# First loads in another order, decay products on ScalarE, two weight units decoded in thirds, and two blocks of tokens taken in turn

## The chip, the cores and the metric

One core of a Trainium2 chip runs the whole kernel. The time is device microseconds (us) of one execution; the kernel before was timed in three runs, and a fourth execution was profiled. Engines are named as in the profile: PE (TensorE; PEld is its weight load), DVE (VectorE), ACT (ScalarE), POOL (GpSimd), SP (the engine that issues most DMAs).

## The reference

The input is a state-space attention layer (4 batches, 8 heads, 768 positions, head size 32, state size 16), then a gated dense layer, then a layer of 8 experts of which each token takes one.

```python
la = log(clip(a)); cum = cumsum(la)                    # per chunk of positions
M  = (C @ B.T) * exp(cum_i - cum_j) * causal
y  = M @ x + (C @ state) * exp(cum)
state = exp(sum(la)) * state + (B * exp(cum_last - cum)).T @ x
X  = y as [3072 tokens, 256]
Z  = ((X @ w_a) * (X @ w_b)) @ w_out                   # w_a, w_b: 256 x 1536, w_out: 1536 x 256
e  = argmax(Z @ w_gate); g = softmax(Z @ w_gate)[e] * sigmoid((Z @ w_output_gate)[e])
out = g * (relu(Z @ w1[e]) @ w2[e])
```

## The kernel before, in words

**Tiles and units.** The 3072 tokens are 24 tiles of 128. Tiles are grouped in blocks (`BLK`, 2 or 4 tiles); blocks 0 and 1 have two tiles each and share one pair of buffers `xh`, `xl`. The dense layer's 1536 inner columns are 12 slices of 128, here called weight units f = 0 to 11. A unit of work (m, f) is block m through slice f: `unit_a` (product `pa` with w_a), `unit_b` (product `pb` with w_b, then the elementwise product and its split into `gh` and `gl`), and later `unit_o` (product `px` with w_out). Each full-precision product is three matmuls, high by high, low by high and high by low (`mm3`). The list `phases` sets the order of the units: block 0 through f = 0 to 2, then blocks 0 and 1 mixed through f = 5, then blocks 2 and 3, and later f = 6 to 11.

**Attention tiles.** `attn_stages(t)` has four steps per tile: `tr` (PE transposes of B and C into `ptr`, ACT evacuates them to `cd` and `BT`), `cb` (PE scores `pcb`, or `pcx` for tile 0; DVE multiplies them by the masked decays `lm` into `mt`), and `ys` (PE `py` or `pyx`; ACT writes `xh`, DVE writes `xl` and the state `Sst`). The decays come from `decays`: DVE scans `a`, and small per-row products follow. `pairs` makes rows 4 to 7 of a tile `q`; `parts` makes the products `A`, `Eb` and `all` (96x4 or smaller) out of `T`; `ends` makes rows 1 to 3 of `q` from them. `ex` transposes rows of `q` on PE and ACT evacuates them into `EX`. `prep` scales B and C by rows of `EX` (`cp`, `Cq`, `Bq`) and makes `lm` by a select on POOL.

**Weights.** They arrive as 64-bit floats, a pair of 32-bit words each. `load_w(f)` issues three loads into one `raw` buffer (w_a, w_b, w_out; three such buffers rotate). `split_w(f)` decodes them in six pieces: `shifted` (ACT, `u`), `low3`, `sign`, `join` (DVE, `raw` and `t`), `hi_w` (ACT, `whi`) and `lo_w` (DVE, `wlo`). Unit 0 is decoded in thirds (256 columns for w_a, then w_b, then w_out); all the others in whole rows of 768 columns.

**What sets the order.** From the first load to the barrier (`tc.no_sync_barrier`) the order on ACT, DVE, POOL and PE is the order in which the code is written. Behind it a scheduler places the instructions of the main loop on each engine. The loop records work unit by unit: a `tick` after each part of a unit brings in attention steps at a rate `PACE`, background steps (`bgstep`, two a tick) and decode steps from the list `dq` at a rate `RATE`; a unit that needs a slice not yet in `decoded` first brings in decode steps until it is there. Each engine executes its own list strictly in order. SP's list holds the loads of B and C (`BCin`, two buffers), of x (`xin`, six buffers) and of weights, each waiting until its buffer is free.

Of the kernel before, what the change touches and what calls it, by code (L numbers as in the profile page):

```python
# [7 lines left out]
F32 = mybir.dt.float32  # L8
# [10 lines left out]
def kernel(  # L19
# [34 lines left out]
    PACE = [2, 2, 2, 2, 1]  # L54
# [111 lines left out]
    def load_bc(u, i):  # L166

        if i == 0:
            BCin[u] = wk.tile([P, 2, G, H, N], F32, tag="BCin", name="BCin")
        b, c = divmod(u * G + i, NCH)  # L170
        for j, src in ((1, B), (0, C)):
            nc.sync.dma_start(out=BCin[u][:, j, i],
                              in_=src[b, :, c * P:(c + 1) * P, :].rearrange("h p n -> p h n"))
# [17 lines left out]
    def decays(r):  # L191
# [88 lines left out]
    def prep(u):  # L280
# [16 lines left out]
        def mul(o, j, qn, eng=None):  # L297
            (eng or nc.gpsimd).tensor_tensor(out=st[o], in0=BCin[u][:, j], in1=bc(qn), op=ALU.mult)

        def lm(i, hf):  # L300
# [4 lines left out]
            for s in range(hf * SUB // 2, (hf + 1) * SUB // 2):  # L305
# [6 lines left out]
        return dict(new=new, cp=lambda: mul("cp", 0, 0), Cq=lambda e=None: mul("Cq", 0, 1, e),  # L312
                    Bq=lambda e=None: mul("Bq", 1, 2, e),
# [123 lines left out]
    def load_w(f):  # L437
        r = stg.tile([P, 3, DM * WD], U32 if wide else F32, tag="raw", name="raw")
        s = slice(f * P * WD, (f + 1) * P * WD)
        for j, src in ((0, w_a), (1, w_b)):  # L440
            v = src.bitcast(U32) if wide else src
# [3 lines left out]
        nc.sync.dma_start(out=r[:, 2, :], in_=v[f * P:(f + 1) * P, :])  # L445
        raws[f] = r

    def split_w(f):
# [7 lines left out]
        def wide_pieces(s):  # L456
# [36 lines left out]
        def narrow_pieces(s):  # L493
            w_ = lambda v: v.rearrange("p j d -> p (j d)")[:, s]

            def hi():
                nc.scalar.activation(out=w_(whi[:, f]), in_=w_(raws[f]), func=AF.Copy)

            def lo():
                V.tensor_tensor(out=w_(wlo[:, f]), in0=w_(raws[f]), in1=w_(whi[:, f]).bitcast(F32),  # L500
                                op=ALU.subtract)
                if s.stop == 3 * DM:
                    decoded.add(f)
# [7 lines left out]
        if f == 1:  # L511
            return ps
# [382 lines left out]
    with tc.manual_schedule(engines={ET.Activation, ET.DVE, ET.Pool, ET.PE}):  # L895
        load_a(0)
        load_bc(0, 0)
        consts_early()
        load_x(0)
        load_bc(0, 1)  # L900
        load_x(1)
        load_w(0)
# [14 lines left out]
        RATE = [1.2, 0.6, 0.3, 0.4, 0.8]  # L917
# [7 lines left out]
        dq = split_w(1) + [more_w]  # L925
# [83 lines left out]
        wa, wb, wo = first  # L1009
# [56 lines left out]
    phases = [(mf(0, range(3)), 1, ()),  # L1066
              ([(0, 3), (1, 0), (1, 1), (0, 4), (1, 2), (1, 3), (0, 5), (1, 4), (1, 5)], 2, ()),
# [102 lines left out]
    for n in range(NU + LAG):  # L1170
# [358 lines left out]
```

## Time and profile before

| | |
|---|---|
| three timed runs | 614.42, 617.46 (median), 619.43 us |
| profiled execution | 617.15 us, of which 615.5 us is the span from the first to the last instruction |
| mean granted TensorE clock | 0.985 of full speed |
| PE matmul busy | 572.7 us, 93% of the span |
| DVE, POOL, ACT busy | 331.1, 250.7 and 243.1 us |

Times in the trace count from the start of the span. In a row, the first numbers are start and duration; what stands in square brackets is how long the engine sat idle before it and whose result it waited for. "x8" means that eight instructions of the same kind are merged in a row, with their busy time together.

### The profile page before, as it was taken

The numbers are of one execution on the slowest core, as the hardware profiler recorded it, in microseconds if no ns is written. First come the engines' busy times: TensorE is split into PE (matmuls) and PEld (weight loads), VectorE is DVE, ScalarE is ACT, GpSimd is POOL, SyncE is SP. The second block draws the span as 40 slices with busy tenths as digits, with TensorE's granted clock in tenths as the row PEclk, the third lists the DMA queues.
The fourth block names the chain that finished last, engine by engine and source line by source line (L and its number), as shares of the span: only waits on it lengthen the run. The fifth ranks groups of instructions, "written<-read, shape, count | busy, mean of one in ns | idle before, by whom it ended". The sixth has DMA issues, their size and how long they took to land. (4 is left out here: it accounts for less than half of the span.)

```text
span 615.5 us, 11171 instructions
## 1 busy us (share of the span) xinstructions
PE 572.7 (93%) x4188; PEld 498.5 (81%) x4188; DVE 331.1 (54%) x886; ACT 243.1 (39%) x533; POOL 250.7 (41%) x327
## 2 busy tenths in 40 slices
PE   2689989999999999999999999999799999999991
PEld 1357879998887777777777789999798898999991
DVE  6879996236644533434233335454847546746720
ACT  2336554344333333333333233435335435435530
POOL 5868446336436432443222322545324332333111
PEclk9999989999999999999999999999979999999997
DMA  8848630003321212120001001403417254154000
GB/s 162 161 107 198 182 39 1 1 5 52 53 26 28 27 27 27 28 36 0 1 1 37 1 1 38 138 20 105 153 44 279 83 182 163 52 179 145 24 22 20
DMA packets 100760, 43.83 MB, mean 71 GB/s; under 512 B 77822, under 2 KB 95432, under 8 KB 100704
## 3 DMA queue, kind: packets, MB, share of 16 engines
q1 hardware_dynamic: 97968, 35.97, 23.3%
q0 software_dynamic: 2736, 7.12, 3.6%
q8 instruction: 34, 0.56, 0.4%
q14 instruction: 22, 0.18, 0.1%
HBM read 36.59 MB, written 6.95 MB: 71 GB/s over the span
## 5 line engine op out<-in xcount | busy, mean ns | idle before, releaser
L517 PE MATMUL pb<-xh,whi 128*128 128x256 f32 (+1 forms) x216 | 72.8, 337 | 1.2 <-ACT as__4669 L534 1.0
L517 PE MATMUL pa<-xh,whi 128*128 128x256 f32 (+1 forms) x216 | 72.0, 333 | 1.6 <-DVE as__875 L544 0.8
L517 PE MATMUL px<-gh,whi 128*128 128x256 f32 (+1 forms) x216 | 71.0, 329 | 0.0
L517 PE MATMUL px<-gl,whi 128*128 128x256 f32 (+1 forms) x216 | 69.4, 321 | 1.0 <-POOL gl L431 1.0
L517 PE MATMUL pa<-xl,whi 128*128 128x256 f32 (+1 forms) x216 | 69.4, 321 | 0.5 <-DVE xl L414 0.5
L517 PE MATMUL px<-gh,wlo 128*128 128x256 f32 (+1 forms) x216 | 69.5, 322 | 0.0
L517 PE MATMUL pa<-xh,wlo 128*128 128x256 f32 (+1 forms) x216 | 69.2, 320 | 0.2 <-DVE wlo L487 0.2
L517 PE MATMUL pb<-xh,wlo 128*128 128x256 f32 (+1 forms) x216 | 69.2, 320 | 0.0
L517 PE MATMUL pb<-xl,whi 128*128 128x256 f32 (+1 forms) x216 | 69.1, 320 | 0.0
L1118 ACT ACTIVATE hh<-ph 128x384 fp32r<-128x384 f32 (+3 forms) x64 | 34.0, 531 | 69.8 <-PE ph L517 52.6
L1119 DVE SCALAR_TENSOR_TENSOR hl<-ph,hh 128x384 fp32r<-128x384 f32 (+3 forms) x64 | 38.7, 605 | 39.1 <-ACT hh L1118 32.1
L1138 PE MATMUL py<-eh,hh 128*128 128x256 f32 x200 | 57.1, 285 | 0.7 <-DVE hl L1119 0.4
L1138 PE MATMUL py<-el,hh 128*128 128x256 f32 x200 | 56.1, 281 | 0.0
L1138 PE MATMUL py<-eh,hl 128*128 128x256 f32 x200 | 56.0, 280 | 0.0
L650 POOL DMA_INDIRECT xg<-x2d,gi x28 | 29.8, 1064 | 55.9 <-ACT lgx L665 36.9
L1154 POOL DMA_INDIRECT out_dram<-yo,si x28 | 29.8, 1064 | 54.6 <-ACT yo L1151 47.2
L306 POOL TENSOR_SCALAR_AFFINE_SELECT lm<-EX 128x256 f32<-128x256 f32 x96 | 47.2, 527 | 9.9 <-DVE mt L372 9.9
L517 PEld LDWEIGHTS pb<-xh,whi 128*128 128x128 f32 x216 | 40.9, 189 | 9.9 <-issue 3.6
L517 PEld LDWEIGHTS pa<-xh,whi 128*128 128x128 f32 x216 | 41.1, 190 | 9.3 <-issue 3.4
L517 PEld LDWEIGHTS px<-gh,whi 128*128 128x128 f32 x216 | 41.1, 190 | 5.4 <-issue 2.1
L517 PEld LDWEIGHTS px<-gh,wlo 128*128 128x128 f32 x216 | 41.0, 190 | 4.6 <-issue 1.3
L517 PEld LDWEIGHTS px<-gl,whi 128*128 128x128 f32 x216 | 41.1, 190 | 4.1 <-POOL gl L431 1.2
(689 smaller groups left out, 1419.0 us busy)
## 6 DMA issues: line engine op xcount, KB each, us to landing
raw<-in_moe_w_dram SPq DMA_DIRECT2D x30, 512.0 KB
x2d<-xr SPq DMA_DIRECT2D x12, 272.0 KB
xin<-in_x_dram SPq DMA_DIRECT2D x24, 128.0 KB
raw<-in_moe_w_a_dram SPq DMA_DIRECT2D x12, 256.0 KB
raw<-in_moe_w_b_dram SPq DMA_DIRECT2D x12, 256.0 KB
raw<-in_moe_w_out_dram SPq DMA_DIRECT2D x12, 256.0 KB
BCin<-in_B_dram SPq DMA_DIRECT2D x24, 64.0 KB
BCin<-in_C_dram SPq DMA_DIRECT2D x24, 64.0 KB
```

The lines of the kernel that those rows point to most:

```text
L306: nc.gpsimd.affine_select(out=Lm[t][:, :, s * SP_:(s + 1) * SP_], in_=exq(4 + s, b, c0 + i, 1).to_broadcast([P, H, SP_]), pattern=[[0, H], ...
L517: nc.tensor.matmul(out=out_, lhsT=l_, rhs=r_, start=first and i == 0, stop=last and i == 2, skip_group_check=skip)
L650: nc.gpsimd.indirect_dma_start(out=xg[:, q, :], out_offset=None, in_=x2d[0:nr, :], in_offset=bass.IndirectOffsetOnAxis(ap=sel["gi", i][:, ...
L1118: nc.scalar.activation(out=hh, in_=ph, func=AF.Relu)
L1119: V.scalar_tensor_tensor(out=hl, in0=ph, scalar=0.0, in1=hh.bitcast(F32), op0=ALU.max, op1=ALU.subtract)
L1138: nc.tensor.matmul(out=po, lhsT=l_[:, s_], rhs=r_, start=(f == 0 and j == 0 and q % 2 == 0), stop=(f == NF2 - 1 and j == 2), skip_group_ch ...
L1154: ins = nc.gpsimd.indirect_dma_start(out=out, out_offset=bass.IndirectOffsetOnAxis(ap=si[0:n_], axis=0), in_=yo, in_offset=None, bounds_ch ...
```

## The change

Five things change, all in the code that runs in the first part of the program.

1. **First loads.** C comes before B, the loads of the first unit's w_a, w_b and w_out are issued one by one between those of tiles 0 and 1, and `cp` of unit 0 is computed per tile.
2. **Small decay products.** `parts` and the fill of row 3 of `q` go to ACT (as `Copy` with a scale taken from a column). Before, POOL made the products and DVE the fill, a copy of one value along the row.
3. **Order before the barrier.** `parts` comes ahead of tile 0's `tr`, tile 0's `ys` ahead of tile 1's `cb`; the w_out third of unit 0 leaves the preamble for the list `dq`.
4. **Thirds.** Weight unit 1 is decoded in thirds as well; `decoded` knows w_a and w_b apart from w_out, and `unit_a` waits for the first two only.
5. **Units.** Block 0 takes f = 0 and 1, then blocks 0 and 1: (1,0), (1,1), (0,2), (1,2), (0,3) and so on. The first `PACE` falls from 2 to 0.7, the first `RATE` rises from 1.2 to 2.

```diff
-    PACE = [2, 2, 2, 2, 1]
+    PACE = [0.7, 2, 2, 2, 1]
...
-        def parts(g=None):
-            g = g or V
-            g.tensor_copy(out=A, in_=a0)
+        def parts():
+            def by(t, i):
+                nc.scalar.activation(out=t, in_=t, func=AF.Copy, scale=T[:, i:i + 1])
+            nc.scalar.activation(out=A, in_=a0, func=AF.Copy)
             for i in range(SUB - 1):
-                g.tensor_scalar(out=A[:, i + 1:], in0=A[:, i + 1:], scalar1=T[:, i:i + 1], scalar2=None, op0=ALU.mult)
+                by(A[:, i + 1:], i)
             for i in range(1, SUB):
-                g.tensor_scalar(out=Eb[:, 0:i], in0=Eb[:, 0:i], scalar1=T[:, i:i + 1], scalar2=None, op0=ALU.mult)
-            g.tensor_tensor(out=all_, in0=T[:, 0:1], in1=Eb[:, 0:1], op=ALU.mult)
+                by(Eb[:, 0:i], i)
+            nc.scalar.activation(out=all_, in_=Eb[:, 0:1], func=AF.Copy, scale=T[:, 0:1])
...
-            V.tensor_copy(out=q[:, 3], in_=all_.to_broadcast([NR, P]))
+            nc.scalar.activation(out=q[:, 3], in_=ones[0:NR], func=AF.Copy, scale=all_)
...
-        if f == 0:
+        if f < 2:
             return [pieces(slice(j * DM, (j + 1) * DM)) for j in range(3)]
...
-        load_bc(0, 0)
+        load_bc(0, 0, (0, 1))
         consts_early()
+        load_bc(0, 1, (0,))
+        load_w(0, (0,))
+        load_bc(0, 1, (1,))
         load_x(0)
-        load_bc(0, 1)
+        load_w(0, (1,))
         load_x(1)
-        load_w(0)
+        load_w(0, (2,))
...
-        RATE = [1.2, 0.6, 0.3, 0.4, 0.8]
+        RATE = [2, 0.6, 0.3, 0.4, 0.8]
...
-        dq = split_w(1) + [more_w]
+        second = split_w(1)
+        dq = second[0] + second[1] + first[2] + [more_w] + second[2] + [more_w]
...
-        s0["tr"]()
-        dc["parts"](nc.gpsimd)
+        dc["parts"]()
+        s0["tr"]()
...
-        s1["cb"]()
         s0["ys"](True)
+        s1["cb"]()
...
-    phases = [(mf(0, range(3)), 1, ()),
-              ([(0, 3), (1, 0), (1, 1), (0, 4), (1, 2), (1, 3), (0, 5), (1, 4), (1, 5)], 2, ()),
+    phases = [([(0, 0), (0, 1)], 1, ()),
+              ([(1, 0), (1, 1)] + [(m, f) for f in range(2, NE) for m in (0, 1)], 2, ()),
...
-            while f not in decoded:
+            while (f, 0) not in decoded:
                 dstep(1)
```

SP's list, from the load of `a` to the first unit's w_out (`BCin` holds B and C of tiles 0 and 1, `xin` x, `raw` weights), before:

```order
L189 DMA araw<-in_a_dram 96x128
L172 DMA BCin<-in_B_dram 128x8x16
L172 DMA BCin<-in_C_dram 128x8x16
L178 DMA xin<-in_x_dram 128x8x32
L172 DMA BCin<-in_B_dram 128x8x16
L172 DMA BCin<-in_C_dram 128x8x16
L178 DMA xin<-in_x_dram 128x8x32
L442 DMA raw<-in_moe_w_a_dram 128x2x256
L442 DMA raw<-in_moe_w_b_dram 128x2x256
L445 DMA raw<-in_moe_w_out_dram 128x512
```

and now:

```order
L189 DMA araw<-in_a_dram 96x128
L172 DMA BCin<-in_C_dram 128x8x16
L172 DMA BCin<-in_B_dram 128x8x16
L172 DMA BCin<-in_C_dram 128x8x16
L448 DMA raw<-in_moe_w_a_dram 128x2x256
L172 DMA BCin<-in_B_dram 128x8x16
L178 DMA xin<-in_x_dram 128x8x32
L448 DMA raw<-in_moe_w_b_dram 128x2x256
L178 DMA xin<-in_x_dram 128x8x32
L452 DMA raw<-in_moe_w_out_dram 128x512
```

The second C moves from the sixth place to the fourth, w_a of the first unit from the eighth to the fifth; behind these ten the list is the same for the next 25 loads.

ACT's list from the first evacuation of `EX` to the first decode piece `u`, before:

```order
L208 ACTIVATE EX<-pd 128x96
L346 ACTIVATE cd<-ptr,head_81 128x128 x2
L348 ACTIVATE BT<-ptr 128x128
L208 ACTIVATE EX<-pd 128x2x96 x2
L468 ACTIVATE u<-raw 128x256
```

and now:

```order
L208 ACTIVATE EX<-pd 128x96
L245 ACTIVATE A_157<-a_155 96x4
L244 ACTIVATE A_157<-A_157,T_156 96x3
L244 ACTIVATE A_157<-A_157,T_156 96x2
L244 ACTIVATE A_157<-A_157,T_156 96x1
L244 ACTIVATE Eb_158<-Eb_158,T_156 96x1
L244 ACTIVATE Eb_158<-Eb_158,T_156 96x2
L244 ACTIVATE Eb_158<-Eb_158,T_156 96x3
L250 ACTIVATE all_161<-Eb_158,T_156 96x1
L349 ACTIVATE cd<-ptr,head_81 128x128 x2
L351 ACTIVATE BT<-ptr 128x128
L208 ACTIVATE EX<-pd 128x2x96 x2
```

Eight small instructions now stand ahead of tile 0's evacuations; a ninth, the fill of row 3 of `q`, stands right behind them and ahead of `u`.

SP's list further on, where the loads of weight unit 3 stand (w_a, w_b, w_out into `raw`; behind two loads of x), before:

```order
L178 DMA xin<-in_x_dram 128x8x32 x2
L442 DMA raw<-in_moe_w_a_dram 128x2x256
L442 DMA raw<-in_moe_w_b_dram 128x2x256
L445 DMA raw<-in_moe_w_out_dram 128x512
L172 DMA BCin<-in_B_dram 128x8x16
```

and now:

```order
L178 DMA xin<-in_x_dram 128x8x32 x2
L172 DMA BCin<-in_B_dram 128x8x16
L172 DMA BCin<-in_C_dram 128x8x16
L172 DMA BCin<-in_B_dram 128x8x16
L172 DMA BCin<-in_C_dram 128x8x16
L178 DMA xin<-in_x_dram 128x8x32
L448 DMA raw<-in_moe_w_a_dram 128x2x256
L448 DMA raw<-in_moe_w_b_dram 128x2x256
L452 DMA raw<-in_moe_w_out_dram 128x512
```

The loads of unit 3 now stand behind four loads of B and C and one of x.

## Rows read from the trace of the kernel before

**Rows 1.** Windows of the span: length, busy PE, PEld, DVE, ACT, POOL, clock, DMA.

```profile
0.00:10.00 10.00, 2.45 (x14) 1.89 (x15) 4.37 (x26) 3.07 (x8) 3.70 (x18) 1.00 0.71 141
10.00:20.00 10.00, 5.22 (x46) 2.39 (x39) 8.67 (x15) 2.12 (x8) 6.90 (x16) 1.00 0.96 202
20.00:30.00 10.00, 5.36 (x41) 3.92 (x45) 8.38 (x18) 4.43 (x11) 10.00 (x20) 1.00 0.83 126
30.00:40.00 10.00, 8.46 (x54) 5.18 (x50) 7.77 (x15) 4.05 (x8) 6.26 (x11) 1.00 0.56 105
40.00:50.00 10.00, 10.00 (x78) 7.21 (x77) 8.95 (x16) 4.48 (x10) 5.87 (x9) 1.00 0.68 201
50.00:60.00 10.00, 8.99 (x98) 7.25 (x97) 10.00 (x17) 6.38 (x17) 9.11 (x11) 1.00 0.74 147
60.00:70.00 10.00, 9.39 (x80) 8.65 (x79) 10.00 (x16) 4.33 (x9) 5.91 (x6) 1.00 0.64 181
70.00:80.00 10.00, 8.60 (x84) 7.58 (x82) 9.84 (x37) 7.13 (x16) 4.17 (x4) 1.00 0.62 162
...
200.00:300.00 100.00, 99.92 (x618) 76.20 (x617) 41.22 (x111) 33.32 (x70) 38.42 (x49) 1.00 0.14 22
```

**Rows 2.** Timeline: the first unit's matmul, two matmuls later, one DVE product.

```profile
24.02 0.58 PE L517 MATMUL pa<-xh,whi 128*128 128x256 f32 x1 [0.50 <-ACT xh L405]
...
25.52 0.41 PE L517 MATMUL pa<-xh,wlo 128*128 128x256 f32 x1
...
45.46 0.28 PE L517 MATMUL pa<-xh,wlo 128*128 128x256 f32 x1
...
80.41 0.41 DVE L544 TENSOR_TENSOR as__964<-pb,as__964 128x256 f32<-128x256 f32 x1
```

**Rows 3.** Timeline of the preamble on DVE and POOL, and a later copy.

```profile
4.51 0.10 DVE L227 TENSOR_TENSOR T<-a,q 96x4 f32<-96x4 f32 x1
...
7.26 0.64 POOL L298 TENSOR_TENSOR cp<-BCin,EX 128x256 f32<-128x256 f32 x1 [4.90 <-DMA BCin<-in_C_dram]
...
10.58 3.22 POOL L306 TENSOR_SCALAR_AFFINE_SELECT lm<-EX 128x256 f32<-128x256 f32 x8
10.66 3.22 DVE L255 COPY q<-all 96x128 f32<-96x128 f32 x1
...
14.98 0.57 DVE L298 TENSOR_TENSOR Cq<-BCin,EX 128x256 f32<-128x256 f32 x1
...
101.57 0.22 DVE L255 COPY q<-all 96x128 f32<-96x128 f32 x1
```

**Rows 4.** Groups by line and form, whole span: count, busy us, mean ns.

```profile
L346 ACT ACTIVATE cd<-ptr,head 128x128 f32<-128x128 f32 x48 | 15.0, 364 | 12.8 <-PE ptr L342 12.7
L348 ACT ACTIVATE BT<-ptr 128x128 f32<-128x128 f32 x4 | 1.1, 278 | 0.0
L476 DVE SCALAR_TENSOR_TENSOR t<-raw 128x768 uint32<-128x768 uint32 x11 | 11.7, 1075 | 0.0
```

**Rows 5.** Timeline: DVE decode pieces, one alone, one beside POOL's selects.

```profile
14.10 0.43 DVE L476 SCALAR_TENSOR_TENSOR t<-raw 128x256 uint32<-128x256 uint32 x1
...
21.07 5.09 POOL L306 TENSOR_SCALAR_AFFINE_SELECT lm<-EX 128x256 f32<-128x256 f32 x11
...
25.32 0.53 DVE L476 SCALAR_TENSOR_TENSOR t<-raw 128x256 uint32<-128x256 uint32 x1
```

**Rows 6.** Timeline: SP's issues of B and of w_out, and ACT waiting for one.

```profile
34.21 0.37 SPq L172 DMA_DIRECT2D BCin<-in_B_dram  x1
...
38.65 0.46 SPq L445 DMA_DIRECT2D raw<-in_moe_w_out_dram  x1
...
45.68 0.46 SPq L445 DMA_DIRECT2D raw<-in_moe_w_out_dram  x1
...
49.52 0.92 ACT L468 ACTIVATE u<-raw 128x768 f32<-128x768 f32 x1 [0.43 <-DMA raw<-in_moe_w_out_dram]
```

**Rows 7.** Window late in the decode stage, columns as in the first group.

```profile
90.00:92.00 2.00, 2.00 (x12) 2.00 (x11) 2.00 (x5) 1.56 (x3) 0.36 (x1) 0.50 0.00 0
```

More of the change, by code (lines that the diff above doesn't have):

```diff
@@ L164, with load_bc @@
     xin, BCin = {}, {}
-    def load_bc(u, i):
-        if i == 0:
+    def load_bc(u, i, js=(1, 0)):
+        if u not in BCin:
             BCin[u] = wk.tile([P, 2, G, H, N], F32, tag="BCin", name="BCin")
         b, c = divmod(u * G + i, NCH)
-        for j, src in ((1, B), (0, C)):
+        for j in js:
             nc.sync.dma_start(out=BCin[u][:, j, i],
-                              in_=src[b, :, c * P:(c + 1) * P, :].rearrange("h p n -> p h n"))
+                              in_=(C, B)[j][b, :, c * P:(c + 1) * P, :].rearrange("h p n -> p h n"))
     def load_x(t):
@@ L295, in new, with mul @@
                 Bpp[t], Cpp[t] = st["Bq"][:, i], st["Cq"][:, i]
-        def mul(o, j, qn, eng=None):
-            (eng or nc.gpsimd).tensor_tensor(out=st[o], in0=BCin[u][:, j], in1=bc(qn), op=ALU.mult)
+        def mul(o, j, qn, eng=None, i=None):
+            s_ = slice(0, G) if i is None else slice(i, i + 1)
+            (eng or nc.gpsimd).tensor_tensor(out=st[o][:, s_], in0=BCin[u][:, j, s_], in1=bc(qn)[:, s_], op=ALU.mult)
         def lm(i, hf):
@@ L310, in lm @@
                     fill=0.0, base=s * SP_, channel_multiplier=-1)
-        return dict(new=new, cp=lambda: mul("cp", 0, 0), Cq=lambda e=None: mul("Cq", 0, 1, e),
-                    Bq=lambda e=None: mul("Bq", 1, 2, e),
+        return dict(new=new, cp=lambda e=None, i=None: mul("cp", 0, 0, e, i),
+                    Cq=lambda e=None, i=None: mul("Cq", 0, 1, e, i),
+                    Bq=lambda e=None, i=None: mul("Bq", 1, 2, e, i),
                     **{f"l{i}{hf}": lambda i=i, hf=hf: lm(i, hf) for i in range(G) for hf in range(2)})
@@ L435, with load_w @@
     WD = 2 if wide else 1
-    def load_w(f):
-        r = stg.tile([P, 3, DM * WD], U32 if wide else F32, tag="raw", name="raw")
+    def load_w(f, js=None):
+        r = raws[f] if f in raws else stg.tile([P, 3, DM * WD], U32 if wide else F32, tag="raw", name="raw")
         s = slice(f * P * WD, (f + 1) * P * WD)
+        raws[f] = r
         for j, src in ((0, w_a), (1, w_b)):
+            if js is not None and j not in js:
+                continue
             v = src.bitcast(U32) if wide else src
@@ L487, in lo_w @@
                 V.tensor_tensor(out=wl_, in0=st["t"].bitcast(F32), in1=wh_.bitcast(F32), op=ALU.subtract)
+                if s.stop >= 2 * DM:
+                    decoded.add((f, 0))
                 if s.stop == 3 * DM:
-                    decoded.add(f)
+                    decoded.add((f, 1))
             return [shifted, low3, sign, join, hi_w, lo_w]
@@ L501, in lo @@
                                 op=ALU.subtract)
+                if s.stop >= 2 * DM:
+                    decoded.add((f, 0))
                 if s.stop == 3 * DM:
-                    decoded.add(f)
+                    decoded.add((f, 1))
             return [lambda: None] * 4 + [hi, lo]
         pieces = wide_pieces if wide else narrow_pieces
-        if f == 0:
+        if f < 2:
             return [pieces(slice(j * DM, (j + 1) * DM)) for j in range(3)]
         ps = pieces(slice(0, 3 * DM))
-        if f == 1:
-            return ps
         return [lambda: (ps[0](), ps[1]()), lambda: (ps[2](), ps[3]()), ps[4], ps[5]]
@@ L1008 @@
         s0, s1 = st[0], st[1]
-        wa, wb, wo = first
+        wa, wb = first[:2]
         V = nc.vector
@@ L1014 @@
         pr0["new"]()
-        pr0["cp"]()
+        pr0["cp"](None, 0)
+        pr0["cp"](None, 1)
         dc["pairs"]()
+        dc["parts"]()
         s0["tr"]()
-        dc["parts"](nc.gpsimd)
         dc["ex"](4, 2)()
@@ L1022 @@
         pr0["l01"]()
+        dc["ends"]()
         s0["cb"](True)
-        dc["ends"]()
         wa[0]()
@@ L1032 @@
         s1["tr"]()
-        wa[4]()
         s0["mask"]()
         pr0["Bq"](V)
+        wa[4]()
         pr0["l10"]()
@@ L1042 @@
         wb[3]()
+        s0["ys"](True)
         s1["cb"]()
-        s0["ys"](True)
+        wb[4]()
         wa[5]()
-        wb[4]()
-        wb[5]()
-        wo[0]()
         dc["tots"]()
         s1["ys"]()
-        for f_ in wo[1:]:
-            f_()
+        wb[5]()
         ahead(0)
@@ L1209 @@
         while oq and (len(oq) > lag(n) or n >= NU):
+            while (oq[0][1], 1) not in decoded:
+                dstep(1)
             unit_o(*oq.pop(0))
```

4 lines of the change are left out of this document (2 added, 2 removed).

## The prediction

> **What bounds the kernel now.** I read the windows first. From 200 to 300 us TensorE is busy 99.92 of 100 us [rows 1]; such a stretch can only be shifted, so a change in the first 100 us is worth what it takes off the moment from which TensorE runs full. In the first 40 us it is busy only 2.45, 5.22, 5.36 and 8.46 us of every ten [rows 1]. The timeline says when its work proper starts: the first matmul of a weight unit stands at 24.02 us, released by ScalarE's `xh` [rows 2]. What stands before it is a latency chain, so each engine of it has to be looked at in turn. The second thing to see is VectorE: from 50 to 80 us it is busy 10.00, 10.00 and 9.84 us of ten while TensorE is at 8.99, 9.39 and 8.60 [rows 1]. There the decode of the weights, on VectorE, sets the pace. An earlier start of TensorE is therefore kept only as far as VectorE, too, gets its work done earlier; both books have to be drawn up.
>
> **The first book: the chain to the first matmul.** Four steps of it change.
>
> *The loads.* POOL's first `cp` starts at 7.26 us, having idled 4.90 us for C [rows 3]. C of tile 0 is now SP's second load and `cp` is split by tile, so tile 0's half (0.3 us, half of 0.64) can run at about 4.6 us, and its transposes after it. This is not worth 2.7 us by itself, since `T` is there only from 4.61 us [rows 3] and the next step takes ScalarE until then.
>
> *The small products.* On POOL they stand between `cp` and the selects that start at 10.58 us [rows 3]. On ScalarE there are eight, each waiting for the one before on the same data. No row shows a 96x4 instruction of ScalarE. From below I take the 128x128 row without a scale column, 0.278 us, less what 124 columns cost, about 0.2 us; from above the 128x128 row with a column, 0.364 us [rows 4]. Between the two rows the column costs 0.09 us, so I take 0.3 us: 4.6 + 7 x 0.3 = 6.7 us for the last of them (bounds 6.0 to 7.2). Behind them stand `cd` twice, `BT` and two evacuations of `EX`: 2 x 0.364 + 0.278 us, and some 0.5 us for `EX`, give 8.2 us, and the selects can start there instead of at 10.58 us.
>
> *The copy.* VectorE's fill of row 3 takes 3.22 us from 10.66 to 13.88 us, exactly as long as POOL's eight selects beside it; the same copy takes 0.22 us at 101.57 us, where no select stands beside it [rows 3]. So it costs VectorE 3.0 us of waiting, and everything behind it in VectorE's list: the first decode third and then `Cq` at 14.98 us [rows 3]. On ScalarE the fill is one more instruction of about 0.3 us, near 8.5 us. Then rows 1 and 2 are transposed behind tile 0's scores (about 9.1 to 9.7 us), evacuated behind one `u` by 10.0 us, and `Cq` can start at about 10.1 us: 4.9 us earlier.
>
> *The order.* Before, `Cq` to the first matmul takes 24.02 - 14.98 = 9.04 us. With tile 0's `ys` ahead of tile 1's scores, TensorE works on tile 0 while ScalarE still evacuates tile 1; I count 0.8 us for it (0 to 1.2). The first matmul then stands at 10.1 + 9.0 - 0.8 = 18.3 us, 5.7 us earlier.
>
> The second load of B, of x and the first weights are moved too, but SP issues the same 35 loads ahead of the place where the lists part again. DMA is busy 0.96 of the window from 10 to 20 us [rows 1], so what comes later in that list (B and C of tiles 2 and 3) lands no earlier than before. By the chain above they are asked for only after 20 us, and cost nothing.
>
> **The second book: VectorE.** I follow it to `as__964` at 80.41 us, the product of the first unit of block 2 [rows 2]. In both orders it has the same work ahead of it: twelve units of blocks 0 and 1 and the decode up to the same piece. VectorE is busy 4.37 + 8.67 + 8.38 + 7.77 + 8.95 + 10.00 + 10.00 + 9.84 = 67.98 us of the first 80 and idle 12.0 us [rows 1]. Of the busy time 3.2 us is the copy, which goes. Thirds add: one piece of 768 columns is 1.075 us [rows 4], three of 256 columns are 3 x 0.43 = 1.29 us [rows 5], so 0.2 us for each of four pieces of one unit, 0.8 us (0 to 1.2). That leaves 65.6 us of work. Idle time: some 6 us until the first matmul (the start, `w_a` on its way, the wait for `Cq`, tile 1's scores), about 2 us less than before, and behind it I take 2.8 us (0.5 to 5), where before there were nearly 4, because more decode work now stands ready between two attention tiles. 65.6 + 6.0 + 2.8 = 74.4 us against 80.0: 5.6 us. The two books agree, and the stricter counts.
>
> The alternating units, PACE and RATE change which unit runs in a gap, not the sum of work; blocks 0 and 1 in turn need a new weight slice only every second unit. I cost this at nothing by itself: it is what holds the middle idle time at 2.8 us, and without that cover it would be 5, a gain of 3.4 us.
>
> Behind 80 us the lists run on in the same order on TensorE and nearly so on the others, and the shift passes through. The profiled execution took 617.15 us, so the forecast is 617.15 - 5.6 = 611.55, say 611.6 us. Its own time lies 0.3 us under the median of 617.46 us, well inside the runs' spread.
>
> **The rivals.**
>
> *Hidden by VectorE.* TensorE starts 5.7 us earlier but VectorE's idle time only moves: of the 12.0 us nothing is saved, and the gain is the copy less the thirds, 3.0 - 0.8 = 2.2 us, 614.9 us. For it speaks that VectorE is full from 50 to 80 us [rows 1]; against it that over 5 us of its idle time lie in the first ten, where the chain gets shorter.
>
> *The stall moves to the next instruction.* The selects now run from about 8.2 us, beside `sign`, `join` and `Cq`. If these were held through all eight selects as the copy was, `Cq` would start near 11.5 + 0.9 us instead of 10.1, and the gain falls to about 3.3 us: 613.9 us. Against it: a decode piece of 256 columns beside the selects took 0.53 us, one beside no select 0.43 us [rows 5], so it waits for a part of one select, 0.1 us, not for a run of them. The Trainium skill, page "SBUF — State Buffer", section "Who interferes with whom", holds that a VectorE instruction with two inputs in SBUF contends with a POOL instruction that reads SBUF, and that whichever issues first keeps the shared port for its whole instruction. That would allow a delay of one select each at least, and the trace agrees in kind, with 0.1 us.
>
> *The clock helps.* In the first 45 us TensorE's matmuls run at the lower level: 256 columns take 0.41 us at 25.52 and 0.28 us at 45.46 us [rows 2], though the granted column reads 1.00. A denser list could bring the change of level forward. And from 90 to 92 us the granted clock is 0.50, that is 1.2 instead of 2.4 GHz [rows 7]; without such a drop another 1 to 2 us go. Gain about 8 us, 609.1 us. Against it: while VectorE sets the pace a faster TensorE only waits longer.
>
> *Slower: the loads of weight unit 3.* They now stand behind four loads of B and C and one of x in SP's list. The first of these waits until tile 3's transposes have freed its buffer. Before, such a series took from 34.21 to 38.65 us from the first B to w_out [rows 6], and a w_out issued at 45.68 us landed at about 49.5 us, where ScalarE had waited for it 0.43 us [rows 6]. So with tile 3's transposes near 26.3 us unit 3 lands at 26.3 + 4.4 + 3.8 = 34.5 us, and is needed near 37 us. ScalarE works in order: if it lands later, `u` holds up the `cd` and `xh` behind it, and every us counts in full. Break-even is at 37 + 5.6, about 43 us; at 45.5 us the kernel takes 620 us. For it: 2.5 us of slack is not much, and other loads have the same place in the list; against it: 8 us more than such a series took before.
>
> **How the numbers follow.** Forecast 0.50, with its own range of 609.6 to 613.8 us (3.4 to 7.5 us: the bounds of the middle idle time, thirds and small products); hidden by VectorE 0.20; the moved stall 0.07; the clock 0.16; slower 0.07. A measurement of this kernel can tell about 1%, 6.2 us, from no change; that mark, near 611.3 us, lies close to the forecast. Faster by more: four tenths of the forecast's 0.50, and most of the clock's 0.16, 0.36 or, with the median 0.3 us above the profiled run, 0.38. Slower by over 1%: 0.05, most of the last rival. Within: 0.57. The range is 607.0 to 616.5 us: below it lies a part of the clock's case, above it the slower one and some of the second's.
>
> **What would show it.** Right: first unit matmul near 18.3 us; no fill on VectorE, a 0.3 us one on ScalarE near 8.5; `Cq` near 10.1; the first product of block 2 near 74.8 us. Wrong: that product above 78 us though the first matmul is early (VectorE hid it); `sign`, `join` or `Cq` of 1 us or more beside the selects; ScalarE idle for a `raw` load; a first matmul after 20 us.

## The result, and the profile after

| | before | after |
|---|---|---|
| median of four runs | 618.34 us | 609.33 us (607.89 to 609.68) |
| profiled execution, its span | 617.15, 615.5 us | 608.97, 607.2 us |
| first matmul of a weight unit | 24.02 us | 17.43 us |
| first product of block 2 | 80.41 us | 74.07 us |

(The four runs of before are the three shown above and one of 619.21 us; the profiled execution of before is not among them, that of the kernel after is.) The ratio is 0.9861, with a 95% interval of 0.9813 to 0.9909: faster, by 1.4%. The forecast was 611.6 us; the change in the profiled executions is 8.2 us instead of 5.6.

Timeline of the kernel after, in the order ScalarE, GpSimd, VectorE, TensorE; the rows answer to [rows 2, 3].

```profile
4.84 0.95 ACT L244 ACTIVATE A<-A,T 96x3 f32<-96x3 f32 x3 [0.19 <-DVE T L227]
...
6.67 0.29 ACT L250 ACTIVATE all<-Eb,T 96x1 f32<-96x1 f32 x1
7.94 0.41 ACT L256 ACTIVATE q<-ones,all 96x128 f32<-96x128 f32 x1
...
4.64 0.41 POOL L300 TENSOR_TENSOR cp<-BCin,EX 128x128 f32<-128x128 f32 x1 [2.29 <-ACT EX L208]
...
7.92 3.67 POOL L308 TENSOR_SCALAR_AFFINE_SELECT lm<-EX 128x256 f32<-128x256 f32 x8 [1.86 <-ACT EX L208]
...
8.70 0.43 DVE L486 SCALAR_TENSOR_TENSOR t<-u,t 128x256 uint32<-128x256 uint32 x1 [0.73 <-ACT u L474]
10.03 0.46 DVE L300 TENSOR_TENSOR Cq<-BCin,EX 128x256 f32<-128x256 f32 x1 [0.90 <-ACT EX L208]
...
74.07 0.41 DVE L552 TENSOR_TENSOR as__975<-pb,as__975 128x256 f32<-128x256 f32 x1
...
17.43 0.58 PE L525 MATMUL pa<-xh,whi 128*128 128x256 f32 x1 [0.50 <-ACT xh L408]
...
41.66 0.41 PE L525 MATMUL pa<-xh,wlo 128*128 128x256 f32 x1
45.22 0.28 PE L525 MATMUL pb<-xh,wlo 128*128 128x256 f32 x1
```

The preamble went almost as counted: the last small product ends near 7.0 us (forecast 6.7), the selects start at 7.92 (8.2), `Cq` at 10.03 (10.1), the first matmul at 17.43 (18.3). The last two rows show that TensorE takes 0.41 us for 256 columns until some 42 us, and 0.28 from 45 us on, as late as before.

Windows of the kernel after, columns as in [rows 1].

```profile
10.00:20.00 10.00, 7.06 (x71) 4.49 (x72) 8.31 (x23) 3.93 (x12) 4.35 (x10) 0.86 1.01 221
20.00:30.00 10.00, 8.13 (x54) 5.14 (x53) 10.00 (x21) 5.34 (x15) 10.00 (x18) 0.50 0.80 98
30.00:40.00 10.00, 10.00 (x59) 7.34 (x60) 8.18 (x15) 3.70 (x9) 9.37 (x19) 0.50 0.80 193
40.00:50.00 10.00, 10.00 (x91) 7.91 (x91) 7.65 (x14) 4.68 (x11) 5.63 (x8) 0.78 0.76 156
50.00:60.00 10.00, 9.29 (x92) 8.55 (x85) 9.89 (x15) 6.10 (x15) 8.28 (x9) 1.00 0.54 154
60.00:70.00 10.00, 9.04 (x71) 8.23 (x70) 10.00 (x16) 6.28 (x13) 3.25 (x4) 1.00 0.67 208
70.00:80.00 10.00, 8.21 (x102) 6.61 (x101) 10.00 (x38) 5.66 (x15) 4.58 (x6) 1.00 0.69 136
...
90.00:92.00 2.00, 2.00 (x19) 2.00 (x19) 2.00 (x8) 0.93 (x3) 1.74 (x2) 1.00 0.00 0
```

From 20 to 50 us TensorE is busy 28.1 of 30 us, against 23.8 [rows 1], at the granted clock of 0.50 until 44 us, and VectorE idles 4.2 us there (4.9 before). From 50 to 80 us VectorE is full, as before. The last row answers to [rows 7]: the fall of the clock at 90 us is gone.

The time does not go in one place. Counting the products of `pb` on VectorE, which come in the same number (108) in both kernels, the 13th (first of block 2) is 6.34 us earlier, the 15th 5.96, the 23rd 7.86, and from there to the end of the span the gain is about 8 us.

### The profile page after: what moved, and what is told of

Same layout as the page of the kernel before. It is cut to its first block, busy times and chain, and to the rows that moved or that the text cites. A ratio compares the mean times of both kernels' runs of the same rounds, so it can differ in the third digit from the quotient of the medians.

```text
span 607.2 us, 11191 instructions
## 1 busy us (share of the span) xinstructions
PE 573.4 (94%) x4188; PEld 498.7 (82%) x4188; DVE 327.0 (54%) x884; ACT 248.4 (41%) x555; POOL 246.4 (41%) x320
## 5 line engine op out<-in xcount | busy, mean ns | idle before, releaser
L1129 DVE SCALAR_TENSOR_TENSOR hl<-ph,hh 128x384 fp32r<-128x384 f32 (+3 forms) x64 | 38.7, 605 | 39.1 <-ACT hh L1128 29.8
L1164 POOL DMA_INDIRECT out_dram<-yo,si x28 | 29.8, 1064 | 54.3 <-ACT yo L1161 47.2
L525 PEld LDWEIGHTS pa<-xl,whi 128*128 128x128 f32 x216 | 41.4, 192 | 4.4 <-DVE xl L417 1.0
L525 PEld LDWEIGHTS pa<-xh,wlo 128*128 128x128 f32 x216 | 41.4, 192 | 3.3
```

Source lines behind the costliest of these rows:

```text
L525: nc.tensor.matmul(out=out_, lhsT=l_, rhs=r_, start=first and i == 0, stop=last and i == 2, skip_group_check=skip)
L1129: V.scalar_tensor_tensor(out=hl, in0=ph, scalar=0.0, in1=hh.bitcast(F32), op0=ALU.max, op1=ALU.subtract)
L1164: ins = nc.gpsimd.indirect_dma_start(out=out, out_offset=bass.IndirectOffsetOnAxis(ap=si[0:n_], axis=0), in_=yo, in_offset=None, bounds_ch ...
```

## The experiments

e1 and e11 are the kernel before with an edit, e8 and e12 are e5 and e1 with one more, all others the kernel after. The two theories at the start: *two books* (the forecast's own: an earlier chain is worth its time, as VectorE's early idle time goes with it) and *hidden by VectorE* (an earlier start only moves VectorE's idle time).

| run | first matmul | 256 columns in 0.28 us from | decode pieces | product of block 2 | ratio to before (95%) |
|---|---|---|---|---|---|
| before | 24.02 | 45.5 | 38 | 80.41 | |
| after | 17.43 | 45.2 | 34 | 74.07 | 0.9861 (0.9813 to 0.9909) |
| e1_small_alone | 20.72 | 44.4 | 38 | 79.05 | 0.9962 (0.9945 to 0.9979) |
| e2_small_back | 21.88 | 42.9 | 34 | 76.12 | 0.9889 (0.9863 to 0.9916) |
| e3_fill_back | 17.43 | 45.4 | 34 | 73.93 | 0.9834 (0.9812 to 0.9856) |
| e4_loads_back | 20.36 | 40.7 | 34 | 73.93 | 0.9856 (0.9834 to 0.9878) |
| e5_units_back | 18.41 | 47.1 | 36 | 78.33 | 0.9968 (0.9954 to 0.9981) |
| e6_warm | 17.52 | 19.0 | 39 | 73.83 | 0.9873 (0.9854 to 0.9892) |
| e7_chain_back | 24.13 | 34.7 | 34 | 75.14 | 0.9899 (0.9870 to 0.9927) |
| e8_gl_vector | 18.30 | 44.7 | 36 | 75.49 | 0.9870 (0.9837 to 0.9904) |
| e9_thirds_back | 17.39 | 48.5 | 36 | 75.75 | 0.9829 (0.9788 to 0.9870) |
| e10_wlo_pool | 17.34 | 45.4 | 36 | 79.62 | 0.9955 (0.9929 to 0.9981) |
| e11_before_gl | 23.99 | 41.5 | 38 | 77.86 | 0.9982 (0.9963 to 1.0001) |
| e12_small_gl | 20.75 | 49.5 | 38 | 78.40 | 0.9918 (0.9899 to 0.9937) |

Times in us. The third column is the first `xh` by `wlo` matmul of a unit that takes 0.28 us and behind which none takes 0.41 in the first 60 us. (Other matmuls can show the change sooner: in e11 `px` takes 0.28 us from 37.3 us on. In e9 0.28 us stands between 28.4 and 29.8 us as well.) Decode pieces are VectorE's pieces ahead of the product of block 2, in rows of 768 columns, three thirds counted as one. Ratios were measured on several chips, markers in one profile each.

**The small products alone.** In the kernel before:

```diff
+        dc["parts"]()            # on ScalarE, the fill too
         s0["tr"]()
-        dc["parts"](nc.gpsimd)
```

> The kernel before, with only the small decay products and the fill of row 3 moved to ScalarE. Markers of before and after: first matmul of a weight unit 24.02 and 17.43 us, first product of block 2 80.41 and 74.07 us, span 615.5 and 607.2 us. Theory (two books): the loads still release the first cp near 7.3 us, so the selects start near 9.9 us (10.58 before); the copy of 3.2 us leaves VectorE. First matmul near 20.8 us, product of block 2 near 77.3 us, span near 612.4 us. Rival (hidden by VectorE, only the copy counts): the same 77.3 us, so this run gives the copy's share under both. Rival (the small products alone are worth nothing, the loads carry all): first matmul above 23 us, product above 79.5 us.

The chain came as expected (first matmul 20.72 us), the product did not: 79.05 instead of 77.3 us, a gain of 1.4 us out of 3.3. The timeline of this run shows a place where the rest may stay, on TensorE and on GpSimd (e12 tests it):

```profile
36.44 0.41 PE L518 MATMUL px<-gl,whi 128*128 128x256 f32 x1 [3.09 <-POOL gl L432]
...
35.67 0.72 POOL L432 TENSOR_TENSOR gl<-as__351,gh 128x256 fp32r<-128x256 f32 x1
```

In the old order of units the first `px` stands on TensorE ahead of an attention tile's scores, and its `gl` comes from GpSimd, behind that engine's selects and constants. In the kernel before TensorE waited 0.95 us at this place.

**The small products back, the fill back, the loads back.** Three kernels, each the kernel after with one part undone:

```diff
-        dc["parts"]()
         s0["tr"]()
+        dc["parts"](nc.gpsimd)   # e2: and the fill on VectorE
...
-            nc.scalar.activation(out=q[:, 3], in_=ones[0:NR], func=AF.Copy, scale=all_)
+            V.tensor_copy(out=q[:, 3], in_=all_.to_broadcast([NR, P]))   # e3: this alone
...
-        load_bc(0, 1, (0,))
-        load_w(0, (0,))
-        load_bc(0, 1, (1,))
         load_x(0)
-        load_w(0, (1,))
+        load_bc(0, 1)            # e4: the old list of loads, cp whole
         load_x(1)
-        load_w(0, (2,))
+        load_w(0)
...
```

> The kernel after, with the small decay products back on GpSimd behind tile 0's transposes and the fill back on VectorE. Theory (two books): the selects start near 9 us, the fill takes about as long as the selects beside it (3.2 us) and everything behind it on VectorE comes 3.5 us later: Cq near 13.6 us, first matmul near 21 us, product of block 2 near 77.3 us, span near 610.5 us. Rival (chain alone, the early loads and the order carry it): first matmul under 19 us, product under 75.2 us.

> The kernel after, with only the fill of row 3 back on VectorE. Theory: one instruction carries most of part 2; it is held through the eight selects that stand beside it and takes 3 us or more, Cq near 13 us, first matmul near 20.3 us, product of block 2 near 77 us. Rival: the fill was slow in the kernel before because of what stood around it there (the late small products); here it takes 0.2 us and nothing moves (first matmul 17.5, product 74.2 us).

> The kernel after, with the old list of first loads and cp of both tiles in one instruction. cp then starts near 7.3 us instead of 4.64, the selects near 9.9 us instead of 7.92, and the first matmul near 19.4 us instead of 17.43. Theory (two books): VectorE's early idle time grows by the same 2 us and the product of block 2 stands near 76 us, span near 609.2 us. Rival (hidden by VectorE): the product stays at 74.1 to 74.6 us although the first matmul is 2 us later.

Timeline of e2 (GpSimd and VectorE), then of e3 (VectorE):

```profile
8.89 3.22 POOL L307 TENSOR_SCALAR_AFFINE_SELECT lm<-EX 128x256 f32<-128x256 f32 x8
...
8.97 3.22 DVE L255 COPY q<-all 96x128 f32<-96x128 f32 x1
```

```profile
7.07 0.21 DVE L256 COPY q<-all 96x128 f32<-96x128 f32 x1
...
9.94 0.43 DVE L300 TENSOR_TENSOR Cq<-BCin,EX 128x256 f32<-128x256 f32 x1 [1.00 <-ACT EX L208]
```

e2's first matmul came later than the theory said (21.88 us), its product between theory and rival (76.12 us): 2.05 us lost for 4.45 us of delay. e3 went the rival's way: where the small products are early, the fill has its turn before the selects, takes 0.21 us on VectorE, and nothing moves. Its place was never the point; its moment was. e4 decides against the forecast's theory: the first matmul is 2.93 us later, the product stands at 73.93 us, and the ratio (0.9856) is that of the kernel after. The new loads are worth nothing at this marker, as *hidden by VectorE* says. Its reason is not shown, though. The second and third product of `pb` in the kernel after, then in e4 with a later wait (VectorE and ScalarE):

```profile
34.76 0.42 DVE L552 TENSOR_TENSOR as__476<-pb,as__476 128x256 f32<-128x256 f32 x1 [0.15 <-PE pb L525]
...
46.24 0.42 DVE L552 TENSOR_TENSOR as__554<-pb,as__554 128x256 f32<-128x256 f32 x1
```

```profile
37.22 0.42 DVE L552 TENSOR_TENSOR as__475<-pb,as__475 128x256 f32<-128x256 f32 x1 [0.72 <-PE pb L525]
...
45.30 0.41 DVE L552 TENSOR_TENSOR as__553<-pb,as__553 128x256 f32<-128x256 f32 x1
...
53.04 0.91 ACT L474 ACTIVATE u<-raw 128x768 f32<-128x768 f32 x1 [1.30 <-DMA raw<-in_moe_w_out_dram]
54.26 0.42 DVE L552 TENSOR_TENSOR as__741<-pb,as__741 128x256 f32<-128x256 f32 x1 [1.12 <-ACT as__741 L542]
```

e4 is 2.46 us behind the kernel after at the second product, and 0.94 us ahead of it at the third. Windows of the two runs between these products, columns as in [rows 1], the kernel after first:

```profile
30.00:44.00 14.00, 14.00 (x79) 10.25 (x82) 11.42 (x19) 5.27 (x14) 11.79 (x22) 0.50 0.73 184
```

```profile
30.00:44.00 14.00, 14.00 (x130) 10.20 (x123) 11.86 (x23) 8.00 (x19) 10.26 (x19) 1.00 0.85 194
```

TensorE is busy all of the time in both and VectorE is not; but the kernel after gets 79 matmuls done, at the granted clock of 0.50, and e4 130 (256 columns take 0.41 us until 37 us there, and 0.28 from 39 us on). So it is TensorE's slower matmuls that use up the early start here. At the sixth product e4's lead is gone again (54.26 against 53.92 us), as `u` on ScalarE waits for a weight load.

**The units back, the chain back.** e5 is the kernel after with the old units, PACE and RATE; e7 is the kernel after with e2 and e4 together, so that the chain is the old one and the units are new:

```diff
-    PACE = [0.7, 2, 2, 2, 1]
+    PACE = [2, 2, 2, 2, 1]       # e5
...
-        RATE = [2, 0.6, 0.3, 0.4, 0.8]
+        RATE = [1.2, 0.6, 0.3, 0.4, 0.8]
...
-    phases = [([(0, 0), (0, 1)], 1, ()),
-              ([(1, 0), (1, 1)] + [(m, f) for f in range(2, NE) for m in (0, 1)], 2, ()),
+    phases = [(mf(0, range(3)), 1, ()),
+              ([(0, 3), (1, 0), (1, 1), (0, 4), (1, 2), (1, 3), (0, 5), (1, 4), (1, 5)], 2, ()),
```

> The kernel after, with the old order of units, PACE and RATE (the thirds, the loads and the small products stay as after). The first matmul of a weight unit stays at 17.4 us. Theory (the order of units holds the middle idle time of VectorE): VectorE idles 2 us more between 20 and 60 us, product of block 2 near 76 us (74.07 in the kernel after). And if the fall of the clock at 88 to 92 us belongs to the old order of units, it is there again and the thirtieth product stands 1.5 us later still (near 118.5 us against 115.01). Rival (the order costs and gives nothing): product of block 2 near 74 us and the thirtieth near 115 us.

> The kernel after, with both the loads and the small products as before; only the order of the preamble's tail, the thirds and the units stay new. First matmul near 23.5 us (17.43 after, 24.02 before). With the loads alone back the product of block 2 stayed at 73.93 us although the first matmul was at 20.36; with the small products alone back it went to 76.12 with the first matmul at 21.88. Theory (the copy beside the selects is what counts, an earlier start does not): product again near 76.1 to 76.5 us. Rival (from a start later than about 20.5 us on, each us of delay counts in full): product near 77.7 us.

Both theories were too low for e5 (78.33 us), both too high for e7 (75.14). With before and after they make a square. Product of block 2:

| | old units | new units |
|---|---|---|
| old chain | 80.41 (before) | 75.14 (e7) |
| new chain | 78.33 (e5) | 74.07 (after) |

The order of units (with PACE and RATE) is worth 4.3 to 5.3 us, the chain 1.1 to 2.1. (e5 and e7 have the thirds and the new tail of the preamble, before has not; so the smaller figures, differences to the kernel after, are the clean ones.) Further on the order weighs more. At the 30th product (before 122.87, e7 116.27, e5 121.36, after 115.01 us) it is worth 6.4 to 6.6 us and the chain 1.3 to 1.5; in the timed ratios 1.0 to 1.1% and 0.3 to 0.4%. Where e5 loses it, on TensorE, GpSimd and VectorE:

```profile
33.66 0.58 PE L525 MATMUL px<-gl,whi 128*128 128x256 f32 x1 [2.83 <-POOL gl L434]
...
32.88 0.72 POOL L434 TENSOR_TENSOR gl<-as__346,gh 128x256 fp32r<-128x256 f32 x1
...
36.29 0.69 DVE L375 TENSOR_TENSOR mt<-pcb,lm 128x512 f32<-128x512 f32 x1 [4.18 <-PE pcb L371]
```

TensorE stands for `gl`, the scores `pcb` stand behind it, and VectorE idles 4.18 us for them. In the kernel after no matmul waits for a `gl` there. The fall of the clock came back in e5 (0.69 from 80 to 85 us), and its 30th product stands at 121.36 us.

Windows of VectorE's two stretches, up to the first matmul and from there to the product of block 2, in the kernel before, after and e7:

```profile
0.00:24.02 24.02, 9.91 (x81) 5.77 (x81) 16.03 (x49) 6.58 (x19) 14.62 (x42) 1.00 0.84 163
24.02:80.41 56.39, 48.56 (x395) 38.31 (x395) 52.36 (x105) 29.42 (x66) 37.30 (x48) 1.00 0.67 156
```

```profile
0.00:17.43 17.43, 10.00 (x81) 5.21 (x81) 11.64 (x47) 8.63 (x28) 6.28 (x21) 0.99 0.88 156
17.43:74.07 56.64, 51.10 (x395) 40.96 (x395) 52.32 (x111) 28.77 (x69) 40.45 (x61) 0.76 0.73 164
```

```profile
0.00:24.13 24.13, 10.07 (x81) 5.67 (x81) 15.54 (x48) 6.42 (x19) 14.71 (x43) 1.00 0.84 163
24.13:75.14 51.01, 44.24 (x395) 35.85 (x395) 50.40 (x111) 28.74 (x69) 33.80 (x47) 1.00 0.69 158
```

TensorE has the same 395 matmuls to do in the second stretch of each. In e7 it does so in 51.01 us, with VectorE idle only 0.61 us; in the kernel after it takes 56.64 us, with VectorE idle 4.32. TensorE's busy time for them is 51.10 us against 44.24, at a granted clock of 0.76 against 1.00. The 6.7 us of earlier start are given back but for 1.07.

**`gl` of the first unit on VectorE**, in e5, in the kernel before (e11) and in e1 (e12):

```diff
-        split(gh, gl, g, nc.gpsimd)
+        split(gh, gl, g, nc.vector if (m, f) == (0, 0) else nc.gpsimd)
```

> The kernel with the old order of units (first matmul 18.41 us, product of block 2 at 78.33 us), with one more change: gl of the very first unit is made on VectorE instead of GpSimd. In the run before it TensorE stood 2.83 us at the first px, waiting for this gl from GpSimd (which made it at 32.88 us, behind selects and constants), the scores pcb stood behind it, and VectorE idled 4.18 us for them. Theory (the old order puts px ahead of the scores, and GpSimd's list holds both): the wait of TensorE for gl goes, VectorE's idle time before that mt falls from 4.18 us below 1.5 us, and the product of block 2 stands near 75.5 us, most of the 4.3 us that the order of units is worth. Rival (the old order needs the third weight slice too early, and the decode is what waits): VectorE's gap only moves by 2 us or less, product above 77.3 us.

In e8 TensorE's wait is gone, and VectorE's gap is 0.98 us:

```profile
33.00 0.69 DVE L375 TENSOR_TENSOR mt<-pcb,lm 128x512 f32<-128x512 f32 x1 [0.98 <-PE pcb L371]
...
75.49 0.41 DVE L552 TENSOR_TENSOR as__981<-pb,as__981 128x256 f32<-128x256 f32 x1
```

The product stands at 75.49 us, as the theory said: with the new chain, 2.84 of the 4.26 us that the order of units is worth go with this one line. Behind block 2 it gives more: the 30th product stands at 115.83 us (e5 121.36, after 115.01), and the timed ratio, 0.9870, is close to that of the kernel after.

> The kernel before, with the gl of the very first unit on VectorE instead of GpSimd and nothing else. In the kernel before TensorE waits 0.95 us for this gl, and VectorE 1.76 us for the scores behind it; the first matmul stands at 24.02 us, the product of block 2 at 80.41 us. Theory (GpSimd's list is a floor for the first px, which the late chain of the kernel before only just touches): little to win here, 1 to 1.5 us, product near 79.2 us. Rival (moving this gl is worth its 2.8 us whatever stands before it): product near 77.6 us.

> The kernel before with the small decay products and the fill on ScalarE (product of block 2 at 79.05 us, TensorE waiting 3.09 us for the first gl), and with that gl on VectorE as well. Theory: the 3.3 us by which the first matmul came earlier, of which only 1.4 us reached the product of block 2, now pass through: product near 76.2 us. Rival (VectorE's own work absorbs the earlier start): product above 78 us.

Both theories missed. In the kernel before the same line moves the product by 2.55 us, near the rival's figure, though the wait that it removes was 0.95 us; so the line does more than end that wait. The timed runs hardly show it (0.9982; the profiled execution, 608.29 us, was the fastest of twelve with a median of 612.33). In e12 the product stands at 78.40 us, as the rival said: the two edits together gain less there than the `gl` line alone. So the wait for `gl` does not explain all that an early start loses with the old units. In e12 256 columns take 0.41 us until 48 us and VectorE idles 6.4 us behind the first matmul; in e11 0.9 us. By the 30th product e12 is ahead of e11 (119.14 against 119.59 us), and its ratio is the better one: a loss at one marker need not last.

**TensorE kept busy.** The kernel after with 34 matmuls added whose results are overwritten:

```diff
+            if t == 1:
+                warm(8)
...
+            if t in (2, 3):
+                warm(5)
...
+            if k == 0 and m == 0 and f < 2:
+                for _ in range(4):
+                    nc.tensor.matmul(out=pa, lhsT=wpart(0, f, k)[0], rhs=xh[:, k, 0:n], start=True, stop=True)
...                              # the same for pb
```

> The kernel after with 34 extra matmuls that compute nothing that is used (8 ahead of tile 1's py, 5 behind the transposes of tiles 2 and 3 each, 4 repeats of the first product in each of the first four product groups), where TensorE idles between 14 and 26 us. In the kernel after the granted clock is 0.50 from 18 to 44 us and VectorE idles 4 us there, behind TensorE. Theory (the lower clock level is what the middle idle time waits on): the granted clock stays at 1.00 or comes back before 35 us, 256 columns take 0.28 us from then on, VectorE's middle idle time falls below 2 us and the product of block 2 stands near 72 us. Rival (VectorE and the loads set the pace, TensorE's level is hidden): the level rises as early, but the product stays at 73.5 to 74.5 us. If the level does not rise earlier, the extra matmuls cost 1 to 2 us (product near 75.5 us) and nothing is told.

The level came early, but for a fall between 26 and 31 us (and one behind the product, from 74 to 79 us). Windows of this run:

```profile
20.00:30.00 10.00, 6.54 (x52) 5.43 (x55) 9.84 (x18) 4.21 (x13) 10.00 (x19) 0.86 0.89 156
30.00:40.00 10.00, 7.63 (x88) 5.44 (x80) 9.24 (x16) 4.99 (x12) 8.45 (x13) 0.97 0.90 208
40.00:50.00 10.00, 9.42 (x88) 7.43 (x88) 10.00 (x20) 6.10 (x14) 8.46 (x13) 1.00 0.91 204
```

VectorE idles 1.0 us behind the first matmul instead of 4.3, and the product still stands at 73.83 us, the 30th at 115.25 (115.01 after). The rival holds for the end. But 39 decode pieces had been done by the product, five more than in the kernel after, since the scheduler placed the list otherwise: VectorE used the time for pieces that block 2 does not need. What the higher level would give with the same pieces this run does not tell.

**The thirds back**, the kernel after with unit 1 decoded in rows, and **a decode piece moved to GpSimd**:

```diff
-        if f < 2:
+        if f == 0:                # e9
...
+        if f == 1:
+            return [ps[:2], ps[2:4], ps[4:]]
...
-                V.tensor_tensor(out=wl_, in0=st["t"].bitcast(F32), in1=wh_.bitcast(F32), op=ALU.subtract)
+                eng = nc.gpsimd if f in (4, 5, 6) else V      # e10
+                eng.tensor_tensor(out=wl_, in0=st["t"].bitcast(F32), in1=wh_.bitcast(F32), op=ALU.subtract)
```

> The kernel after, with weight unit 1 decoded in whole rows of 768 columns again. Theory: the thirds cost 0.8 us of VectorE's work and buy an earlier second unit; u, hi and the row-wise pieces then stand longer ahead of the evacuations on ScalarE, as in the kernel before, where TensorE waited 2.33 us for BT. Without them the second product comes 2 us or more later than 34.76 us, and the product of block 2 stands 0.5 to 1.5 us later than 74.07 us. Rival (the thirds cost more than they give): product near 73.3 us.

> The kernel after, with the last decode piece (wlo) of weight units 4, 5 and 6 on GpSimd instead of VectorE. From 60 to 80 us GpSimd is busy 3.25 and 4.58 us of ten and VectorE 10.00. Theory (VectorE's work sets the time until TensorE runs full): three pieces of about 0.95 us leave VectorE; products of blocks 2 and later come 2 us earlier, span near 605 us where 607.2 was measured, or below 601 where the same chip gave 602.6. Rival (the engines share a path to the buffers: VectorE's pieces beside a gl of GpSimd take 1.49 us instead of 0.94): VectorE's other pieces grow by as much as it saves, and the product of block 2 stays within 0.7 us of 74.07 us.

e9: the product is 1.68 us later, a little more than expected, but not by the way expected. The second product comes earlier (33.41 us); then TensorE waits for GpSimd again (1.83 us for `gl`), `u` waits 1.45 us for a weight load at 51.81 us, and two more decode pieces stand ahead of block 2. Its timed ratio, 0.9829, does not show the loss, so the price of the thirds stays open within some 2 us. e10 is 5.5 us slower at the product; theory and rival both missed. The pieces take 1.9 to 2.6 us on GpSimd, and VectorE's piece with one input is held beside them:

```profile
66.60 2.55 POOL L494 TENSOR_TENSOR wlo<-t,whi 128x768 fp32r<-128x768 f32 x1 [1.19 <-DVE as__849 L553]
...
67.35 2.22 DVE L478 TENSOR_SCALAR raw<-raw 128x768 uint32<-128x768 uint32 x1
```

## Why the prediction was right, and where it was not

The time fell into the range, but beyond the mark near 611.3 us: over 1% faster, for which the forecast had 0.38, against 0.57 for less than that either way. VectorE's book gave the product of block 2 within 0.7 us (74.07 against 74.8). That agreement is better than its reasons.

**Right, by the markers.** The chain to the first matmul: small products of 0.3 us, `cp` by tile at 4.64 us, selects, `Cq`, and the first matmul 0.9 us earlier than forecast: from `Cq` on the tail took 7.40 us (9.04 before), so the order gave 1.6 us where 0.8 was counted. The moved stall did not come: beside the selects `Cq` took 0.46 us and a decode piece 0.43. The slower case, the loads of weight unit 3, did not come either: no `u` in the first 50 us of the kernel after waited for a load. But the wait itself is real somewhat later: `u` idled for a weight load 0.43 us in the kernel before (49.52 us), 1.30 in e4, 2.71 in e5 (53.66 us) and 1.80 in e8 (50.28 us). In the kernel after it idled 0.58 us at 52.69 us, with no releaser in the trace.

**Wrong: what the early start is worth.** "Some 6 us until the first matmul (...), about 2 us less than before, and behind it I take 2.8 us": the first was 5.79 us, the second 4.32 (4.03 before). I held the two to be independent. In e7, with the old chain, it is 8.59 and 0.61. So for the larger part of the chain the idle time only moved, as the first rival, *hidden by VectorE*, has it; I gave it 0.20. Its reason, a full VectorE, is not what the rows show between the first matmul and the product: the same 395 matmuls keep TensorE busy 44.24 us in e7 and 51.10 in the kernel after, and VectorE idles behind it. What the earlier start gives, TensorE's longer time at the lower level takes back. In e6, with the higher level, VectorE is the full one and the product does not move either; as five more pieces were decoded there, which of the two engines would set the pace stays open.

**Wrong: the order of units "at nothing by itself".** It is worth 4.3 to 5.3 us at the product and over 6 us at the end, the larger part of the whole change. The forecast's case without it was a gain of 3.4 us; e5 keeps 2.08 at the product.

**Wrong: "in both orders it has the same work ahead of it".** Groups of VectorE's decode by form up to the product of block 2, before and after:

```profile
L487 DVE TENSOR_TENSOR wlo<-t,whi 128x768 fp32r<-128x768 f32 x8 | 10.1, 1257 | 0.0
L476 DVE SCALAR_TENSOR_TENSOR t<-raw 128x768 uint32<-128x768 uint32 x9 | 9.9, 1104 | 0.0
L480 DVE SCALAR_TENSOR_TENSOR t<-u,t 128x768 uint32<-128x768 uint32 x8 | 8.7, 1083 | 0.0
L472 DVE TENSOR_SCALAR raw<-raw 128x768 uint32<-128x768 uint32 x9 | 7.9, 884 | 0.0
```

```profile
L482 DVE SCALAR_TENSOR_TENSOR t<-raw 128x768 uint32<-128x768 uint32 x7 | 9.7, 1389 | 0.0
L493 DVE TENSOR_TENSOR wlo<-t,whi 128x768 fp32r<-128x768 f32 x6 | 6.6, 1099 | 0.0
L486 DVE SCALAR_TENSOR_TENSOR t<-u,t 128x768 uint32<-128x768 uint32 x6 | 6.1, 1022 | 0.0
L478 DVE TENSOR_SCALAR raw<-raw 128x768 uint32<-128x768 uint32 x7 | 5.3, 762 | 0.0
```

34 rows before, 26 after; thirds went from 12 to 24, which stands for four rows. One whole weight unit fewer, four pieces of about 1 us, is decoded ahead of block 2. Nothing needs it there: blocks 0 to 3 all work on f up to 5. The unit is paid behind block 2's first product: the last `wlo` ends at 93.9 us (97.0 before). The gain hardly shrinks for it (6.34 us at the 13th product, 5.96 at the 15th, 7.86 at the 23rd). That this is part of what the order is worth follows from the counts; no run changed RATE alone.

**Sized wrongly: the thirds.** Twelve more of them cost 6.9 us of VectorE's durations (13.1 against 6.2) instead of the 4.3 us of four rows: 2.6 us and not 0.8.

**Half right: the clock.** This rival's figure, 609.1 us, is the nearest to what was measured, for half of its reason. The early stage was not helped. The fall at 90 us went, and behind block 2 the kernel gained 1.5 us more than forecast. From the 13th to the 30th product before, e1, e5 and e10, which have such a fall there, take 42.1 to 43.0 us, the nine kernels without one 40.3 to 41.7 (e6, with one and the added matmuls, 41.4); that the fall is the reason is likely, but no run shows it alone. With the old units the three kernels with `gl` of the first unit on GpSimd (before, e1, e5) have it and the three with it on VectorE (e8, e11, e12) have not. What brings it was not settled.

So the sum was right by luck, because errors met: VectorE's idle time was 1.3 us longer than counted (10.1 against 8.8), the thirds cost 1.8 us more, and the units, priced at nothing, took a weight unit of decode and a wait for GpSimd off the path.

## What to carry to other kernels

An earlier start counts only if what it waits for next is earlier as well: undo the start alone and look whether the first common marker moves, before pricing the chain. Compare marker by marker: a lead can be lost at another engine, or to a load, and one marker is not the end. When a list is put in another order, count each engine's instructions up to a marker by form; work decoded ahead of need is paid in the stage where that engine is full. An engine's wait for a small result made on a crowded engine (`gl` on GpSimd) blocks all that stands behind it; look at what stands next in line, not at the wait's own length.

## What the hardware showed that I had not expected

VectorE's fill was held through eight selects in a row (3.22 us in e2, 0.21 in e3, where it came first), while two-input pieces beside selects lost about 0.1 us. In e10 a piece with one input was held for 2.2 us (0.55 at 68.95 us in the kernel after) by one GpSimd instruction. The Trainium skill, page "SBUF — State Buffer", section "Who interferes with whom", says that copies and tensor-scalar operations can enter a mode that takes the shared port, and that the other side is then blocked for a whole instruction; the traces agree in what was held and by whom (no row shows the mode or the port), and add that a run of back-to-back selects can hold the copy through all of them.

TensorE's change from 0.41 to 0.28 us for 256 columns did not follow its start: near 35 us with a first matmul at 24.13 (e7), near 45 with one at 24.02 (before) and with one at 17.43 (after), near 49 with one at 20.75 (e12), though TensorE was busy 28 of the 30 us from 20 to 50 us in the kernel after. With idle stretches filled it was there at 19 us (e6). In the kernel after, with the granted clock at 0.50 until 44 us, this late change is what VectorE's 4.3 us of idle time stand beside; why it comes when it does stays open.
